# A decayed linear attention with two MLPs on one core: pair products by parity in row tiles of TensorE, and two operands turned by its transpose

## The chip, the core and the metric

The kernel runs on one core of one Trainium2 chip. The metric is the device time of one execution in microseconds (us); lower is better. Names used below: TensorE (PE in the profile; its weight loads are PEld), VectorE (DVE), ScalarE (ACT), GpSimd (POOL) and SyncE (SP), whose queue issues nearly all DMAs.

## What is computed

Attention first: for each of 4 x 8 heads a state of 40 x 40 goes through 768 tokens.

```python
for t in range(S):
    y[:, :, t] = np.einsum('bhd,bhde->bhe', rt, state)
    Sa = np.einsum('bhde,bhe->bhd', state, at)
    state_decay = state * wt[:, :, None, :] - np.einsum('bhd,bhe->bhde', Sa, bt)
    state = state_decay + np.einsum('bhd,bhe->bhde', vt, kt)
```

Then y, as 3072 rows of 320, goes through a first MLP, `((x @ w1) * (x @ w2)) @ w3 @ w_out` (width 1024), and a second, `h = x @ w_in; (h * cos(h)) @ w_out` (width 2048). All is float32.

## The kernel before

**Chunks.** The 768 tokens are cut into 24 chunks of C = 32. The 32 heads are kept as NP = 16 pairs: of each pair the even head lies on partitions 64 to 103 (the slice `EV`), the odd one on 0 to 39 (`OD`), D = 40 values of d each. "par" is 0 for even and 1 for odd. Four chunks make a group, whose small triangular systems are solved together.

**Preparation of a chunk** (`prep`, L313). On VectorE: a scan over the decays (L320), a product with k and b (L321, the tile KS, 104 partitions x 16 pairs x 64 columns: 32 of k and 32 of b), a reciprocal and a copy (L326, L327), a second scan (L329, Dp), and two products of a with it, one for each parity (L334), into the tile GA. GA holds, for each pair, 2 x 72 columns: for each parity 32 columns of the product and 40 of an identity, and zeros wherever the rows belong to the other parity. SyncE then issues the load of the next chunk's decays and a (`load_wa`, two DMAs, L282 and L283), and two DMAs that copy the products out of GA into the chunk's slot KA (L339).

**Pair products** (`gstage`, L342), in two halves of 8 pairs. L351: one matmul for each pair, stationary KS (104 rows, 64 columns), moving GA (104 rows, 144 columns). Because of GA's zeros each matmul gives both parities' 32 products, and, through the identity, k and b with tokens on rows. Results are in a PSUM tile PG, of two banks. ScalarE takes them out with 12 copies for each half (L361 into lam, the systems; L362 into KA; L363 into KB), and GpSimd masks KA (L369).

**v times r** (`mv`, L459): 16 matmuls for a chunk (L466), stationary v (104 rows, 32 columns), moving RD (104 rows, 2 x 32 columns, where the other parity's rows are zero). Copies to X (L472), masks (L475).

**The chain.** Chunk after chunk, in halves: `st_z` (L496), `st_q` (L513), `st_u` (L524), `st_y` (L542), `st_s` (L485), small float32 matmuls with copies and products between them on ScalarE, VectorE and GpSimd. It needs KA, KB and X of its chunk and the group's solved systems TT. Systems are solved by `tinv_start` (32 block transposes, L378) and `tinv` (L406, L408, L425, L428 on VectorE, with a share on GpSimd), and handed on by `tfin` (L457).

**The rest.** Between the pieces of the chain stand the first MLP's products (`ab`, L686), the folding of w3 and w_out (L586) and the conversion of weights from 64-bit words (L160 to L162). Phase 2 (`x2`, `hh`, `oo`, L736 to L798) follows.

**Order.** `attention` writes out the start by hand: chunks 0 to 3 are prepared and their systems solved, then chunks 4 and 5. From then on pieces are emitted by due times (`time`, constants START and PACE), which are their priorities too, and a list scheduler sets each engine's own order from that, with a model of its own for how long things take. Every engine then runs its list strictly in order, SyncE's queue too.

Of the kernel before, what the change touches and what calls it, by code (L numbers as in the profile page):

```python
# [9 lines left out]
F32 = mybir.dt.float32  # L10
# [42 lines left out]
def host_layout(inp):  # L53
# [20 lines left out]
    cst = np.zeros((128, 112 + NP * (C + 1)), np.float32)  # L74
    cst[OD, 0:D] = np.eye(D)
    cst[EV, 0:D] = np.eye(D)
    cst[:, 40:80] = 1.0
    cst[:, 80:112] = np.arange(128)[:, None] % 32 + np.arange(C)[None] >= C
    cst[:, 112::C + 1] = 1.0
# [15 lines left out]
class Room:  # L95
    """Buffers by tag, each in its turn, in places that something else has left."""
# [19 lines left out]
class Kernel:  # L116
# [25 lines left out]
    # ---------------------------------------------------------------- float64 words to float32  # L142
# [31 lines left out]
    # ---------------------------------------------------------------- attention  # L174
# [4 lines left out]
    def attn_open(self, ctx):  # L179
# [4 lines left out]
        self.ident_m = cp.tile([128, 112], F32, name="ident_m")  # L184
        self.ident = self.ident_m[:, 0:40]
        self.mask = self.ident_m[:, 80:112].unsqueeze(1)
        self.mask72 = self.ident_m[:, 40:112].unsqueeze(1)
# [10 lines left out]
        self.XX = t(104, [2, NP, 72], "Xe")  # L198
        self.X = [[self.XX[:, i] for i in range(2)], [t(128, [NP, 72], f"Xo{i}") for i in range(2)]]
# [11 lines left out]
    def prep_open(self):  # L211
# [21 lines left out]
        self.GA = [t(104, 2 * NP, 72).rearrange("p (x a) n -> p x a n", x=2), self.XX]  # L233

    def KS(self, c):
        """Of the first chunks in room that the weights will take, then in place."""
        if c >= PRE:
            return self.kb
        n = 2 * NP * C
        return self.ks[c // 2 % 2][0:104, n * (c % 2):n * (c % 2 + 1)].rearrange("p (a n) -> p a n", a=NP)  # L240

    def attn_init(self):
        nc = self.nc
        v, g, a = nc.vector, nc.gpsimd, nc.scalar
        nc.scalar.dma_start(out=self.d1r, in_=self.ap["cst"][0:104, 112:])
        nc.scalar.dma_start(out=self.ident_m, in_=self.ap["cst"][:, 0:112])
# [6 lines left out]
        idb = self.ident.unsqueeze(1)  # L253
        for t, e in zip(self.GA, (v, g)):
            e.memset(t, 0.0)
            a.copy(t[EV, 0, :, 32:72], idb[EV].to_broadcast([D, NP, D]))
            a.copy(t[OD, 1, :, 32:72], idb[OD].to_broadcast([D, NP, D]))
# [4 lines left out]
        for x in self.X[1]:  # L262
            g.memset(x, 0.0)
        for x in self.Dt:
            g.memset(x[32:64], 0.0)

    def attn_init2(self):
        nc = self.nc
        idb = self.ident.unsqueeze(1)
        for i in range(NB):  # L270
            nc.scalar.copy(self.KB[0][i][EV], idb[EV].to_broadcast([D, NP, D]))
            nc.scalar.copy(self.KB[1][i][OD], idb[OD].to_broadcast([D, NP, D]))
        nc.gpsimd.memset(self.XX, 0.0)
        nc.gpsimd.memset(self.RD, 0.0)
        nc.gpsimd.memset(self.vd[32:64], 0.0)
# [38 lines left out]
    def prep(self, c, alt=0):  # L314
# [3 lines left out]
        Dt, KS, GA = self.Dp, self.KS(c), self.GA[alt]  # L318
# [14 lines left out]
        for par, R in ((0, EV), (1, OD)):  # L333
            v.tensor_tensor(out=GA[R, par, :, 0:C], in0=self.a[R], in1=Dt[R], op=ALU.mult)  # L334
# [3 lines left out]
        for par, R in ((0, EV), (1, OD)):  # L338
            nc.sync.dma_start(out=self.KA[par][s][R], in_=GA[R, par, :, 0:C])  # L339
        yield  # L340

    def gstage(self, c, hf, alt=0, P=None):  # L342
# [3 lines left out]
        GA, KS = self.GA[alt], self.KS(c)  # L346
        for q in range(2):
            for e in range(2):
                for ct in range(2):
                    p = 8 * hf + 4 * q + 2 * ct + e  # L350
                    nc.tensor.matmul(P[64 * ct:64 * ct + 64, q, 144 * e:144 * e + 144], lhsT=KS[:, p, :], rhs=GA[:, :, p, :], start=True, stop=True)  # L351
        s, ci = c % NB, (c + OFF) % GC
        lam = self.lam.rearrange("p t (c f q e) -> p f q e t c", c=GC, f=2, q=2)
        pairs = lambda t: t[:, 8 * hf:8 * hf + 8].rearrange("p (q c e) n -> p c q e n", q=2, c=2)
        for ct in range(2):
            o = 64 * ct
            Pv = P[o:o + 64, :, 0:288].rearrange("p q (e x n) -> p x q e n", e=2, x=2)
            for par in range(2):
# [12 lines left out]
    def tinv_start(self):  # L371
        """Systems by partition: transpose blocks of lambda, and minus the identity."""
# [10 lines left out]
    def quads(t, row, col, *dims):  # L383
        """Both diagonal blocks of a matrix in halves, from a row and a column of the block on."""
        return bass.AP(tensor=t.tensor, offset=t.offset + 32 * row + 16 + col, ap=[t.ap[0], [496, 2], *dims])

    def tinv(self):
        """Minus the inverses, by halves of the tokens: both diagonal blocks by forward substitution, then the block
        between them as the product of the three; the first QD columns of a half on one engine, the others on another.
        Products before their sums lie in blocks of the systems that are done with."""  # L390
# [20 lines left out]
        def product(e, q0, q1, out, a, b):  # L411
            """out(q)[q, i], the sum over k of a[i, k] b(q)[q, k]."""
# [46 lines left out]
    def mv(self, c):  # L459
# [3 lines left out]
        for i in range(4):  # L463
            for ct in range(4):
                o = 288 + 64 * (i % 2)
                nc.tensor.matmul(P[32 * ct:32 * ct + 32, i // 2, o:o + 64], lhsT=self.vd[:, 4 * i + ct, :], rhs=RD[:, :, 4 * i + ct, :], start=True, stop=True)  # L466
        for ct in range(4):
            Pv = P[32 * ct:32 * ct + 32, :, 288:416].rearrange("p b (i x n) -> p x b i n", i=2, x=2)
            for par in range(2):
                o = 64 * par  # L470
                X = self.X[par][c % 2][o:o + 32, :, D:72].rearrange("p (b i c) n -> p c b i n", b=2, c=4)
                nc.scalar.copy(X[:, ct], Pv[:, par])  # L472
# [4 lines left out]
    def st_s(self, c, hf):  # L477
        """State rows by d for the next chunk's first stage, columns still to be scaled."""
# [128 lines left out]
    def w12(self, c):  # L607
        """256 columns of w1 and w2: both parts of two tiles of rows, and those of the 64 rows left over as one tile."""
# [40 lines left out]
    # ---------------------------------------------------------------- MLP  # L649
# [22 lines left out]
    def ab(self, s, x, f):  # L672
        """p for one tile of 128 hidden columns."""
# [33 lines left out]
    def load_p(self, s):  # L707
        """The parts of p, high and low."""
# [11 lines left out]
    def x2(self, s):  # L720
        """x2 by whole tiles of columns, then the rest with its two parts of weights as one tile."""
# [135 lines left out]
    def weights_b(self):  # L857
        """Weights of what follows, in the room of the attention's preparation."""
# [21 lines left out]
    def weights_c(self):  # L880
        """Weights of the last part, in the room of the last chunks as each ends."""
# [41 lines left out]
    def attention(self):  # L923
# [6 lines left out]
        for c in range(GC - OFF):  # L930
            for _ in self.prep(c, c % 2):
                pass
            for hf in range(2):
                self.gstage(c, hf, c % 2, halves[hf])
# [14 lines left out]
        for c in range(GC - OFF, PRE):  # L949
            for _ in self.prep(c):  # L950
                pass
            for hf in range(2):
                self.gstage(c, hf, 0, halves[hf])
# [52 lines left out]
    def back(self):  # L1006
        """The chunks' preparation, as far ahead as there is room, and each group's systems."""
# [89 lines left out]
```

## Time and profile before

| what | us |
|---|---|
| three runs | 1217.88, 1225.14, 1231.16 |
| median of the runs | 1225.14 |
| span of the profiled execution | 1225.8 |
| TensorE busy, of the span | 1054.0 |
| VectorE busy | 822.7 |
| ScalarE busy | 666.5 |
| GpSimd busy | 590.3 |
| mean granted TensorE clock | 0.919 of full speed |

The profiled execution thus stands 0.7 us above the median. A row of a group reads: line, engine, operation, tile written <- tiles read, shapes, count | busy us, mean ns of one | idle time before them and what ended it. A float32 matmul of the program stands in the trace as two matmuls and two weight loads; an fp32r matmul (the MLPs and the fold) as one. Ends of matmuls are modelled, with a latency of some 0.2 us in each, so starts are what paces are read from.

### The profile page before, as it was taken

The page shows a single profiled execution, that of the slowest core. Times are in us where ns is not written, and L with a number is a line of the kernel's source. Part 1 is how long each engine was busy: PE and PEld are TensorE (multiplying, and loading weights), DVE is VectorE, ACT ScalarE, POOL GpSimd, SP SyncE. Part 2 cuts the span into 40 slices and gives each one's busy share as a digit, 9 for nine tenths or more (in the row PEclk, how much of TensorE's full clock was granted, in tenths as well). Part 3 has the DMA queues.
Part 4 walks back from the last instruction along what each step waited for, and adds up shares of the span by engine and source line. Part 5 has one row for each costly group of instructions (what it writes and reads, how often), then busy time and mean ns, then how long its engine had stood idle before and what let it go on. Part 6 is the DMA issues. An engine that isn't in the chain of part 4 may idle for free. (4 is left out here: it accounts for less than half of the span.)

```text
span 1225.8 us, 34181 instructions
## 1 busy us (share of the span) xinstructions
PE 1054.0 (86%) x13536; PEld 954.3 (78%) x13536; DVE 822.7 (67%) x1774; ACT 666.5 (54%) x1750; POOL 590.3 (48%) x734
## 2 busy tenths in 40 slices
PE   2332558889999899999989999999999999999997
PEld 2322457767777777778877777899999999999997
DVE  5677799789769878976966666555455555455554
ACT  7653546646773765658435543455545555545453
POOL 7227557337345643734546654554334444334333
PEclk9755669899989999989989798999999999999999
DMA  5532545454554465454465545311101111101000
GB/s 133 137 86 67 144 118 150 136 145 116 162 144 123 129 159 148 118 160 119 136 202 160 142 140 166 119 35 46 46 21 37 46 36 47 45 20 38 12 4 20
DMA packets 137446, 122.96 MB, mean 100 GB/s; under 512 B 67293, under 2 KB 113885, under 8 KB 135749
## 3 DMA queue, kind: packets, MB, share of 16 engines
q1 hardware_dynamic: 137024, 120.49, 35.0%
q8 instruction: 106, 1.74, 0.6%
q14 instruction: 55, 0.45, 0.1%
q10 hardware_dynamic: 261, 0.28, 0.1%
HBM read 87.17 MB, written 29.62 MB: 95 GB/s over the span
## 5 line engine op out<-in xcount | busy, mean ns | idle before, releaser
L782 POOL TENSOR_TENSOR w<-w,w 128x512 fp32r<-128x512 f32 x96 | 126.1, 1321 | 224.8 <-ACT w L781 224.8
L686 PE MATMUL ab<-xh,w 128*128 128x256 f32 x960 | 177.7, 316 | 9.1 <-DVE p L691 8.5
L686 PEld LDWEIGHTS ab<-xh,w 128*128 128x128 f32 x960 | 135.7, 201 | 32.9 <-DVE p L691 10.1
L774 DVE SCALAR_TENSOR_TENSOR w<-w,h 128x512 f32<-128x512 int32 x96 | 65.7, 685 | 134.7 <-ACT w L772 120.0
L770 PE MATMUL h<-x2h,r 128*128 128x256 f32 x720 | 139.9, 280 | 1.3 <-ACT x2h L746 1.2
L776 ACT ACTIVATE w<-w,hpi 128x512 f32<-128x512 f32 x96 | 69.5, 724 | 93.1 <-DVE w L775 92.9
L770 PEld LDWEIGHTS h<-x2h,r 128*128 128x128 f32 x720 | 115.7, 188 | 1.8 <-ACT x2h L746 1.7
L778 DVE TENSOR_TENSOR w<-h,w 128x512 f32<-128x512 f32 x96 | 66.2, 689 | 65.5 <-ACT w L776 65.5
L361 ACT COPY sh<-PG 32x128 f32<-32x128 f32 x168 | 63.3, 377 | 50.9 <-PE PG L351 49.1
L690 ACT COPY p<-ab 128x256 f32<-128x256 f32 x96 | 35.8, 373 | 100.5 <-PE ab L686 85.5
L772 ACT ACTIVATE w<-h 128x512 int32<-128x512 f32 x96 | 57.1, 596 | 58.4 <-PE h L770 58.3
L775 DVE SCALAR_TENSOR_TENSOR w<-w 128x512 f32<-128x512 int32 x96 | 83.7, 871 | 3.3
L542 PE MATMUL PY<-Xe,r 104*40 104x72 f32 x768 | 69.3, 247 | 18.1 <-DVE Dt L554 9.6
L369 POOL TENSOR_SCALAR_AFFINE_SELECT r<-r 32x512 f32<-32x512 f32 x48 | 45.7, 952 | 79.7 <-ACT r L362 77.8
L686 PE MATMUL ab<-xl,w 128*128 128x256 f32 x384 | 82.2, 297 | 0.0
L770 PE MATMUL h<-x2l,r 128*128 128x256 f32 x288 | 79.8, 279 | 0.0
L781 ACT CAST w<-w 128x512 fp32r<-128x512 f32 x96 | 59.4, 619 | 34.6 <-DVE w L778 34.6
L542 PEld LDWEIGHTS PY<-Xe,r 104*40 104x40 f32 x768 | 58.1, 130 | 22.1 <-POOL Xe L533 6.1
L686 PE MATMUL ab<-xr,w 64*128 64x256 f32 x192 | 75.2, 395 | 0.0
L351 PE MATMUL PG<-sh 104*64 104x144 f32 x576 | 52.0, 322 | 22.2 <-issue 6.9
L542 PE MATMUL PY<-Xo,r 128*40 128x72 f32 x768 | 65.2, 246 | 1.3 <-POOL Xo L533 0.7
L686 PEld LDWEIGHTS ab<-xl,w 128*128 128x128 f32 x384 | 63.6, 203 | 1.0 <-issue 0.4
(218 smaller groups left out, 3428.3 us busy)
## 6 DMA issues: line engine op xcount, KB each, us to landing
pd<-p SPq DMA_DIRECT2D x96, 128.0 KB
sh<-wa SPq DMA_DIRECT2D x48, 242.5 KB
f<-w3t SPq DMA_DIRECT2D x32, 256.0 KB
sh<-kb SPq DMA_DIRECT2D x48, 160.0 KB
pl<-pd SPq DMA_DIRECT2D x6, 1024.0 KB
w<-pd SPq DMA_DIRECT2D x6, 1024.0 KB
w34d<-f SPq DMA_DIRECT2D x32, 160.0 KB
r<-wo SPq DMA_DIRECT2D x16, 320.0 KB
```

What stands on the lines that cost most here:

```text
L351: nc.tensor.matmul(P[64 * ct:64 * ct + 64, q, 144 * e:144 * e + 144], lhsT=KS[:, p, :], rhs=GA[:, :, p, :], start=True, stop=True)
L361: nc.scalar.copy(lam[32 * j:32 * j + 32, hf, :, :, :, ci], Pv[32:64, par, :, :, 0:C])
L542: nc.tensor.matmul(P[o:o + D, i // 4, 72 * (i % 4):72 * (i % 4) + 72], lhsT=self.KB[par][s][0:K, p, :], rhs=self.X[par][c % 2][0:K, p, :], ...
L686: nc.tensor.matmul(P[:, w], lhsT=l_, rhs=r_, start=(n == 0), stop=(n == len(ops) - 1))
L770: nc.tensor.matmul(P[:, q], lhsT=l_, rhs=r_, start=(n == 0), stop=(n == len(ops) - 1))
L772: a.activation(out=k, in_=P, func=ACTF.Copy, scale=1.0 / (2 * math.pi), bias=0.25)
L774: v.scalar_tensor_tensor(out=r, in0=k, scalar=-C1, in1=P, op0=ALU.mult, op1=ALU.add)
L775: v.scalar_tensor_tensor(out=r, in0=k, scalar=-C2, in1=r, op0=ALU.mult, op1=ALU.add)
L776: a.activation(out=r, in_=r, func=ACTF.Sin, bias=self.hpi)
L778: v.tensor_tensor(out=gt, in0=P, in1=r, op=ALU.mult)
L781: a.copy(gh, gt)
L782: g.tensor_tensor(out=gl, in0=gt, in1=gh.bitcast(F32), op=ALU.subtract)
```

## The change

`prep` writes a times Dp straight into the slot KA (contiguous rows of 40 x 512); GA, its zeros, its identities and the two copying DMAs (L339) go. `gstage` has two matmuls for a pair in place of one: the rows of one parity only (40 rows, 64 columns of KS, 32 columns moving), with the parities in different row tiles of TensorE and in different banks of PG. The identity part is replaced by four transposes in a half, each of two pairs of KS at once (104 rows x 128 columns in, 128 x 104 out, one 104 x 104 identity). `mv` likewise has 32 matmuls of 40 rows and 32 moving columns in place of 16 of 104 rows and 64. ScalarE's copies keep their number and sizes; they read other columns. At the start, GA's memsets and four identity copies go, X's zeros are set once.

```diff
@@ prep
-        for par, R in ((0, EV), (1, OD)):
-            v.tensor_tensor(out=GA[R, par, :, 0:C], in0=self.a[R], in1=Dt[R], op=ALU.mult)
+        for par, R in ((0, EV), (1, OD)):
+            v.tensor_tensor(out=self.KA[par][s][R], in0=self.a[R], in1=Dt[R], op=ALU.mult)
             if par == 0:
                 yield
         self.load_wa(c + 1)
-        for par, R in ((0, EV), (1, OD)):
-            nc.sync.dma_start(out=self.KA[par][s][R], in_=GA[R, par, :, 0:C])
@@ gstage
         for q in range(2):
             for e in range(2):
+                i = 2 * q + e
                 for ct in range(2):
                     p = 8 * hf + 4 * q + 2 * ct + e
-                    nc.tensor.matmul(P[64 * ct:64 * ct + 64, q, 144 * e:144 * e + 144], lhsT=KS[:, p, :], rhs=GA[:, :, p, :], start=True, stop=True)
+                    for par, R in ((0, EV), (1, OD)):
+                        nc.tensor.matmul(P[64 * ct:64 * ct + 64, par, C * i:C * i + C], lhsT=KS[R, p, :],
+                                         rhs=self.KA[par][s][R, p, :], start=True, stop=True)
+        for q in range(2):
+            for ct in range(2):
+                p = 8 * hf + 4 * q + 2 * ct
+                o = 128 + 104 * ct
+                nc.tensor.transpose(P[:, q, o:o + 104], KS[:, p:p + 2, :].rearrange("p a n -> p (a n)"), self.ident)
...
-                nc.scalar.copy(lam[32 * j:32 * j + 32, hf, :, :, :, ci], Pv[32:64, par, :, :, 0:C])
-                nc.scalar.copy(pairs(self.KA[par][s][r:r + 32])[:, ct], Pv[0:32, par, :, :, 0:C])
-                nc.scalar.copy(pairs(self.KB[par][s][r:r + 64])[:, ct], Pv[:, par, :, :, C:72])
+                nc.scalar.copy(lam[32 * j:32 * j + 32, hf, :, :, :, ci], Pv[32:64, par])
+                nc.scalar.copy(pairs(self.KA[par][s][r:r + 32])[:, ct], Pv[0:32, par])
+                nc.scalar.copy(odd(self.KB[par][s][r:r + 64])[:, ct], Pt[:, :, :, R])
@@ mv
         for i in range(4):
+            o = 336 + C * i
             for ct in range(4):
-                o = 288 + 64 * (i % 2)
-                nc.tensor.matmul(P[32 * ct:32 * ct + 32, i // 2, o:o + 64], lhsT=self.vd[:, 4 * i + ct, :], rhs=RD[:, :, 4 * i + ct, :], start=True, stop=True)
+                for par, R in ((0, EV), (1, OD)):
+                    nc.tensor.matmul(P[32 * ct:32 * ct + 32, par, o:o + C], lhsT=self.vd[R, 4 * i + ct, :], rhs=RD[R, par, 4 * i + ct, :], start=True, stop=True)
```

The list scheduler makes a new order of all this. Two engines and three places matter below.

SyncE, at the load of chunk 5's decays (`wa`, a DMA for each parity; `dtd` is Dp going out, r the slot that holds KA), before:

```order
L331 DMA dtd_99<-Dp 40x512 x2
L282 DMA sh_170<-wa 40x1552
L282 DMA vd<-vd 40x512
L309 DMA Xe<-vt 32x16x40 x2
L283 DMA vd<-vd 40x512
L304 DMA rd<-rd 40x512 x2
L283 DMA sh_170<-wa 40x1552
L339 DMA r<-sh_170 40x16x32 x2
```

and with the change:

```order
L315 DMA dtd_99<-Dp 40x512 x2
L266 DMA sh_171<-wa 40x1552
L267 DMA sh_171<-wa 40x1552
L266 DMA vd<-vd 40x512
L267 DMA vd<-vd 40x512
L288 DMA rd<-rd 40x512 x2
```

The second half of the load stood behind six other DMAs and now follows the first at once; the copies into the slot are gone.

VectorE, at the same time, from the block transposes of the first group's systems (x32) on, before:

```order
L378 STREAM_TRANSPOSE sh_171<-sh_170 128x32 x32
L406 TENSOR_TENSOR sh_171<-sh_171,sh_170 128x2x15
L408 TENSOR_TENSOR sh_170<-sh_170,sh_171 128x2x15
L406 TENSOR_TENSOR sh_171<-sh_171,sh_170 128x4x14
L408 TENSOR_TENSOR sh_170<-sh_170,sh_171 128x2x2x14
L406 TENSOR_TENSOR sh_171<-sh_171,sh_170 128x6x13
L408 TENSOR_TENSOR sh_170<-sh_170,sh_171 128x2x3x13
L320 SCALAR_TENSOR_TENSOR sh_170<-sh_170 104x528
```

and with the change:

```order
L371 STREAM_TRANSPOSE sh_172<-sh_171 128x32 x32
L304 SCALAR_TENSOR_TENSOR sh_171<-sh_171 104x528
L399 TENSOR_TENSOR sh_172<-sh_172,sh_171 128x2x15
L305 TENSOR_TENSOR w_176<-sh_171 104x2x16x32
L310 RECIPROCAL sh_172<-sh_171 104x16
L401 TENSOR_TENSOR sh_171<-sh_171,sh_172 128x2x15
```

The scan that waits for the load (L320, now L304) has moved ahead of six steps of the solution.

TensorE, at the 40th half of the pair products (the last but eight of all 48), before:

```order
L542 MATMUL PY<-Xe,r 40x72
L542 MATMUL PY<-Xo_147,r 40x72
L496 MATMUL PC_167<-rd,Ssb 40x64
L496 MATMUL PC_168<-rd,Ssb 40x64 x7
L351 MATMUL PG<-sh_170 64x144 x8
L496 MATMUL PC_168<-rd,Ssb 40x64
L586 MATMUL f<-f_751,f_753 128x320 x2
```

and with the change (L506 is `st_q`):

```order
L506 MATMUL PC_168<-Xe_147,r 32x72
L506 MATMUL PC_168<-Xo_149,r 32x72
L336 MATMUL PG<-r,sh_171 64x32 x16
L342 MATMUL PG<-ident,sh_171 128x104 x4
L506 MATMUL PC_169<-Xe_147,r 32x72
L506 MATMUL PC_169<-Xo_149,r 32x72
```

Eight matmuls of one shape have become sixteen and four, in two tilings of the array. Before, the neighbours L496 used the same tiling (all rows, 64 columns); now the tiling changes on entering, in the middle and on leaving.

More of the change, by code (lines that the diff above doesn't have):

```diff
@@ L73, in host_layout @@
     wf[..., 1:] = dmaj(w)[..., :-1]
[L74 to L79, printed above, removed]
+    cst = np.zeros((104, 104 + NP * (C + 1)), np.float32)
+    cst[:, 0:104] = np.eye(104)
+    cst[:, 104::C + 1] = 1.0
     return {
@@ L183, in attn_open @@
         self.ap_ = cp
[L184 to L187, printed above, removed]
+        self.ident = cp.tile([104, 104], F32, name="ident")
         t = lambda p, f, nm: cp.tile([p] + f, F32, name=nm)
@@ L197, in attn_open @@
         self.Dt = [t(104, [NP, C], f"Dt{i}") for i in range(ND)]
-        self.XX = t(104, [2, NP, 72], "Xe")
-        self.X = [[self.XX[:, i] for i in range(2)], [t(128, [NP, 72], f"Xo{i}") for i in range(2)]]
+        self.X = [[t(104, [NP, 72], f"Xe{i}") for i in range(2)], [t(128, [NP, 72], f"Xo{i}") for i in range(2)]]
         self.WC = [t(104, [NP], f"WC{i}") for i in range(NB + 1)]
@@ L244, in attn_init @@
         v, g, a = nc.vector, nc.gpsimd, nc.scalar
-        nc.scalar.dma_start(out=self.d1r, in_=self.ap["cst"][0:104, 112:])
-        nc.scalar.dma_start(out=self.ident_m, in_=self.ap["cst"][:, 0:112])
+        nc.scalar.dma_start(out=self.d1r, in_=self.ap["cst"][:, 104:])
+        nc.scalar.dma_start(out=self.ident, in_=self.ap["cst"][:, 0:104])
         v.memset(self.wa[32:64], 0.5)
@@ L252, in attn_init @@
         g.memset(self.lam, 0.0)
[L253 to L257, printed above, removed]
         for i in range(NB):
@@ L261, in attn_init @@
             g.memset(self.KB[1][i][0:64], 0.0)
-        for x in self.X[1]:
+        for x in self.X[0] + self.X[1]:
             g.memset(x, 0.0)
@@ L268, in attn_init2 @@
         nc = self.nc
[L269 removed]
         for i in range(NB):
[L271 to L273 removed]
+            for par, R in ((0, EV), (1, OD)):
+                nc.scalar.copy(self.KB[par][i][R], self.ident[R, R].unsqueeze(1).to_broadcast([D, NP, D]))
         nc.gpsimd.memset(self.RD, 0.0)
[L275 removed]
         for t in self.PC:
@@ L312, in load_vt, with prep @@
                 )
-    def prep(self, c, alt=0):
+    def prep(self, c):
         nc = self.nc
@@ L317, in prep @@
         s = c % NB
-        Dt, KS, GA = self.Dp, self.KS(c), self.GA[alt]
+        Dt, KS = self.Dp, self.KS(c)
         fl = lambda x: x.rearrange("p a t -> p (a t)")
@@ L337, in prep, with gstage @@
         self.load_wa(c + 1)
-        for par, R in ((0, EV), (1, OD)):
-            nc.sync.dma_start(out=self.KA[par][s][R], in_=GA[R, par, :, 0:C])
         yield
-    def gstage(self, c, hf, alt=0, P=None):
+    def gstage(self, c, hf, P=None):
         nc = self.nc
         P = P or self.PG
-        GA, KS = self.GA[alt], self.KS(c)
+        KS, s = self.KS(c), c % NB
         for q in range(2):
             for e in range(2):
+                i = 2 * q + e
                 for ct in range(2):
@@ L355, in gstage @@
         for ct in range(2):
             o = 64 * ct
-            Pv = P[o:o + 64, :, 0:288].rearrange("p q (e x n) -> p x q e n", e=2, x=2)
-            for par in range(2):
+            Pv = P[o:o + 64, :, 0:128].rearrange("p x (q e n) -> p x q e n", q=2, e=2)
+            Pt = P[o:o + 64, :, 128:336].rearrange("p q (c n) -> p q c n", c=2)
+            for par, R in ((0, EV), (1, OD)):
                 r = 64 * par
                 j = 2 * par + ct
-                nc.scalar.copy(lam[32 * j:32 * j + 32, hf, :, :, :, ci], Pv[32:64, par, :, :, 0:C])
-                nc.scalar.copy(pairs(self.KA[par][s][r:r + 32])[:, ct], Pv[0:32, par, :, :, 0:C])
-                nc.scalar.copy(pairs(self.KB[par][s][r:r + 64])[:, ct], Pv[:, par, :, :, C:72])
+                nc.scalar.copy(lam[32 * j:32 * j + 32, hf, :, :, :, ci], Pv[32:64, par])
+                nc.scalar.copy(pairs(self.KA[par][s][r:r + 32])[:, ct], Pv[0:32, par])
+                nc.scalar.copy(odd(self.KB[par][s][r:r + 64])[:, ct], Pt[:, :, :, R])
@@ L463, in mv @@
         for i in range(4):
+            o = 336 + C * i
             for ct in range(4):
-                o = 288 + 64 * (i % 2)
-                nc.tensor.matmul(P[32 * ct:32 * ct + 32, i // 2, o:o + 64], lhsT=self.vd[:, 4 * i + ct, :], rhs=RD[:, :, 4 * i + ct, :], start=True, stop=True)
+                for par, R in ((0, EV), (1, OD)):
+                    nc.tensor.matmul(P[32 * ct:32 * ct + 32, par, o:o + C], lhsT=self.vd[R, 4 * i + ct, :], rhs=RD[R, par, 4 * i + ct, :], start=True, stop=True)
         for ct in range(4):
-            Pv = P[32 * ct:32 * ct + 32, :, 288:416].rearrange("p b (i x n) -> p x b i n", i=2, x=2)
             for par in range(2):
                 o = 64 * par
-                X = self.X[par][c % 2][o:o + 32, :, D:72].rearrange("p (b i c) n -> p c b i n", b=2, c=4)
-                nc.scalar.copy(X[:, ct], Pv[:, par])
+                X = self.X[par][c % 2][o:o + 32, :, D:72].rearrange("p (i c) n -> p c i n", c=4)
+                nc.scalar.copy(X[:, ct], P[32 * ct:32 * ct + 32, par, 336:464].rearrange("p (i n) -> p i n", n=C))
         for par in range(2):
@@ L930, in attention @@
         for c in range(GC - OFF):
-            for _ in self.prep(c, c % 2):
+            for _ in self.prep(c):
                 pass
             for hf in range(2):
-                self.gstage(c, hf, c % 2, halves[hf])
+                self.gstage(c, hf, halves[hf])
         for _ in self.tinv_start():
@@ L952, in attention @@
             for hf in range(2):
-                self.gstage(c, hf, 0, halves[hf])
+                self.gstage(c, hf, halves[hf])
         self.ready |= {("tfin", 0), ("mv", 0)}
```

4 lines of the change are left out of this document (2 added, 2 removed).

## Prediction

> **What bounds the kernel now.** First the page's busy tenths in 40 slices of 30.6 us.
>
> ```profile
> PE   2332558889999899999989999999999999999997
> DVE  5677799789769878976966666555455555455554
> ACT  7653546646773765658435543455545555545453
> PEclk9755669899989999989989798999999999999999
> ```
>
> Three stretches show. In the first 120 us TensorE is a third busy at a low granted clock, and VectorE leads. From some 200 to 785 us TensorE is nearly full beside a busy VectorE. From 785 us on it is full, and the change touches nothing there. The stages in numbers (PE, PEld, DVE, ACT, POOL; clock; DMA):
>
> ```profile
> core 0: us, PE busy (x) PEld busy (x) DVE busy (x) ACT busy (x) POOL busy (x), PEclk, DMA share, GB/s
> 100.00:200.00 100.00, 52.95 (x1101) 46.33 (x1098) 84.34 (x224) 44.38 (x137) 61.68 (x92) 0.66 0.44 117
> 200.00:300.00 100.00, 87.61 (x1521) 73.30 (x1521) 85.68 (x221) 62.72 (x198) 52.00 (x77) 0.95 0.46 129
> 400.00:500.00 100.00, 90.04 (x1646) 75.23 (x1646) 82.72 (x216) 64.23 (x207) 48.08 (x69) 1.00 0.54 147
> 600.00:700.00 100.00, 91.54 (x1636) 76.84 (x1636) 67.17 (x148) 49.27 (x138) 62.80 (x91) 0.88 0.59 171
> 900.00:1000.00 100.00, 100.00 (x786) 99.96 (x785) 48.95 (x72) 52.12 (x93) 39.27 (x31) 1.00 0.14 43
> ```
>
> So in the middle TensorE's own time sets the end for nine tenths: a microsecond more or less on its list is worth about 0.9. At the start it is VectorE's list up to the first solved systems, for which the chain waits (total, times, longest, in us):
>
> ```profile
> PEld PC L524 <- DVE TT L457: 15.7, 1, 15.7
> ```
>
> **TensorE's paces.** Its list around 406 to 413 us (start, length, count), and the v-times-r products at 654 us:
>
> ```profile
> 406.04 1.20 PE L351 MATMUL PG<-sh 104*64 104x144 f32 x16
> 411.13 0.73 PE L524 MATMUL PC<-Q,TT 32*32 32x72 f32 x32 [1.54 <-ACT Q L515]
> 412.19 0.75 PE L686 MATMUL ab<-xh,w 128*128 128x256 f32 x5
> 412.78 0.40 PE L686 MATMUL ab<-xl,w 128*128 128x256 f32 x2
> 413.11 0.38 PE L686 MATMUL ab<-xr,w 64*128 64x256 f32 x1
> 413.42 0.50 PE L686 MATMUL ab<-xh,w 128*128 128x256 f32 x2
> 654.69 0.65 PE L466 MATMUL PG<-rd,vd 104*32 104x64 f32 x32
> ```
>
> Durations, minimum/median/maximum in ns, and when the group ran:
>
> ```profile
> L351 PE MATMUL PG<-sh x576: 283/286/503, 83.5 to 571.3; 104*64 104x144 f32 x192
> L351 PEld LDWEIGHTS PG<-sh x576: 132/137/231, 83.4 to 571.2; 104*64 104x64 f32 x192
> L513 PEld LDWEIGHTS PC<-Xe,r x768: 106/110/178, 62.0 to 717.2; 104*32 104x32 f32 x192
> L524 PE MATMUL PC<-Q,TT x1536: 221/221/329, 115.5 to 723.7; 32*32 32x72 f32 x192
> L686 PEld LDWEIGHTS ab<-xh,w x960: 186/188/338, 185.1 to 776.6; 128*128 128x128 f32 x192
> L466 PE MATMUL PG<-rd,vd x768: 216/219/317, 53.2 to 695.8; 104*32 104x64 f32 x192
> ```
>
> Taking the last one's latency off a run and dividing by the steps: L351 (1.20 - 0.29) / 15 = 61 ns a record, L524 (0.73 - 0.22) / 31 = 16 ns, L466 (0.65 - 0.22) / 31 = 14 ns. L351 uses two tiles of 64 columns in turn, the others four tiles. If tiles run beside each other, one record takes 121 ns for 144 moving columns, 66 for 72, 56 for 64: always 0.84 to 0.91 ns a column. 32 columns should take 28 ns. A weight load grows from 110 ns at 32 columns to 188 at 128, 0.81 ns a column: 52 ns for 64 columns, 104 for 128, if the rest is latency. In the full array an fp32r record goes at (412.78 - 412.19) / 5 = 0.118 us for 256 columns. From the first xl to the 64-row xr it is 0.33 us, so the second xl took 0.21: a **change of tiling** costs 0.09 us.
>
> **The change on TensorE, half by half.** Removed: 16 records at 61 ns, 0.97 us.
>
> Added, products: 32 records in four tiles (two row tiles, two column tiles), eight rounds. A round takes 28 ns if the streams decide (0.22 us in all), 52 if the 64-column loads do (0.42), and 16 rounds of 52 if two row tiles over the same columns don't run together (0.83). L524's four tiles lie on a diagonal, so no row shows row tiles sharing columns. I take 0.42: loads must go on, and L351's gaps have never tested one that is longer than its stream.
>
> Added, transposes: four with 128-column loads. The trace has none. From below, 104 columns at the full array's pace, 48 ns each (0.19 us); from above, two records each like other float32 work here, both load-bound (8 x 104 = 0.83). I take one record, load-bound, 0.42, as L686's 32-bit words go in one record. The Trainium skill ("TensorE: Matmul & The Clock Gate", Terms) has a transpose mode four times as fast for float32; by it the 0.42 would stand, and no run so far shows one.
>
> So a half takes 0.84 (0.41 to 1.66) for 0.97. From 83 to 571 us there are 576 / 16 = 36 halves: -4.7 us (-20 to +25).
>
> **v times r.** Now 32 records x 14 ns = 0.45 us a chunk. Then 64 records of 28 ns: 0.45 if four run at once, as now, 0.22 if all eight tiles do, 64 x 14 = 0.90 if the 14 ns are a price of each record. I take 0.45: nothing (for some 20 chunks in the middle, -5 to +9 us).
>
> **Tilings.** The transposes stand in the full array between products in 64 x 64 tiles, and `st_s`, `st_y`, `st_z` no longer share a tiling with them. Counted over TensorE's order from the first `st_q` to the last `st_y`, the tiling changes 590 times before and 696 times after. 106 x 0.09 = +9.5 us.
>
> Together +4.8 us on TensorE (-25 + 9.5 = -15 at best, +25 + 9 + 9.5 = +43 at worst). At 0.9 of it: **+4.3 us** (-14 to +39).
>
> **The change at the start.** VectorE's list around the first systems (brackets: idle before, and what ended it):
>
> ```profile
> 57.86 3.07 DVE L378 STREAM_TRANSPOSE sh<-sh 128x32 f32<-128x32 f32 x32
> 65.65 1.26 DVE L320 TENSOR_TENSOR_SCAN sh<-sh 104x528 f32<-104x528 f32 x1 [3.04 <-DMA sh<-wa]
> 76.77 1.26 DVE L320 TENSOR_TENSOR_SCAN sh<-sh 104x528 f32<-104x528 f32 x1 [2.12 <-DMA sh<-wa]
> 88.36 1.26 DVE L320 TENSOR_TENSOR_SCAN sh<-sh 104x528 f32<-104x528 f32 x1 [2.94 <-DMA sh<-wa]
> 101.49 1.26 DVE L320 TENSOR_TENSOR_SCAN sh<-sh 104x528 f32<-104x528 f32 x1 [2.56 <-DMA sh<-wa]
> 113.57 1.90 DVE L457 STREAM_TRANSPOSE TT<-sh 128x1024 f32<-128x1024 f32 x1
> ```
>
> And SyncE's queue, start and length of each issue, at the load that the first of these scans waits for:
>
> ```profile
> 56.86 0.30 SPq L282 DMA_DIRECT2D sh<-wa  x1
> 57.26 0.79 SPq L282 DMA_DIRECT2D vd<-vd  x1
> 60.91 0.28 SPq L283 DMA_DIRECT2D sh<-wa  x1
> 61.24 1.73 SPq L339 DMA_DIRECT2D r<-sh  x2
> ```
>
> The scans wait 10.7 us there. The first is late because the load's second half is issued at 60.91, behind vd, vt and rd; scan and issue lie 4.7 us apart. With the halves side by side it starts near 57.3 + 4.7 = 62.0, one microsecond after the transposes end (60.9) and not three to five. The fourth scan now has the rest of the first solution step and five products of the next ahead of it, which cover its load. The two between keep their waits. That leaves 1 + 2.1 + 2.9 + 0 = 6 of 10.7 us, so TT is ready **5 us** earlier (0 to 7: GpSimd's share of the solution might be what is late next), and VectorE, 84% busy until 200 us, hands it on.
>
> **Costed at nothing.** The copies L339 took 1.73 us of SyncE's queue for a chunk; no compute instruction in the middle waited for them, and they were not on the way to the end. VectorE's product keeps its size. GA's memsets and identities lie under the first load of decays. ScalarE's copies read as many columns. If SyncE's relief does help, it is a microsecond or two.
>
> Sum: 1225.8 + 4.3 - 5 = **1225 us**, within 0.1 us of the runs' median of 1225.1. The likeliest case's own range is 1214 to 1237; a measurement of this kernel tells about 1% (12 us) from no change.
>
> **Rivals.**
>
> *Row tiles overlap and little else costs (chance 0.25).* Streams decide, not loads, transposes go at the full array's pace, eight tiles run at once: -14 us on TensorE's list as above, -5 at the start, so 1207. For it: the paces fit streams everywhere. Against: the tiling changes are certain.
>
> *TensorE pays by the record (0.20): slower.* The place is the stream of short records in `gstage` and `mv`: 32 and 64 records where 16 and 32 stood. If products go two at a time behind 64-column loads (0.83) and `mv` keeps 14 ns a record (0.90), then (0.83 + 0.42 - 0.97) x 36 = +10, +9 and +9.5: 28.5 x 0.9 - 5 = +21, so 1246. It decides from some 20 ns a product record on. For it: no record here goes below 14 ns on average. Against: 14 and 16 ns fit streams of 56 and 66 ns in four tiles.
>
> The Trainium skill ("TensorE: Matmul & The Clock Gate", the section "Wait — 56ns, not 53.3ns?") states that starts never follow closer than about 25 ns. As a rule for all tiles together (0.03) it would make 32 x 25 = 0.80 and 64 x 25 = 1.6 us: +9, +23 and +9.5, times 0.9, less 5: 1258. L524's 16 ns and L466's 14 ns speak against it.
>
> *It does not reach the end (0.10).* TensorE's list isn't what binds where the halves stand, since VectorE is 80% busy beside it; only the start counts: 1221, still no change.
>
> **How the numbers follow.** Forecast 0.42 at 1225, hidden 0.10 at 1221: no change beyond 1% (1213 to 1237) has 0.52. Faster has 0.25, slower 0.20 + 0.03 = 0.23. The range takes in the first two rivals, 1206 to 1248.
>
> **What would show it.** Right: a half's products near 0.4 us plus latency and four transposes near 0.4; `mv` still near 0.65 us; 100 more changes of tiling; the transposition into TT (L457 before) near 108 us; phase 2 as long as before. Wrong: products at 1 us a half, eight transpose records a half, `mv` above 1 us, or TT when it was. A span that moves with none of these would mean that the new order, and not these costs, decides.

## The result, and the profile after

The changed kernel takes 1288.1 us in the median of four runs (1275.4 to 1293.4), the kernel before 1228.2 us beside it (1217.9 to 1237.2). The ratio is 1.047, with a 95% interval of 1.041 to 1.054: slower by 60 us, where 1225 us was forecast and 1248 was the end of the range. Here and below medians are over all runs of a kernel and ratios over its fast runs alone, so the two can differ by some tenths of a per cent.

Where the time lies is seen in the busy tenths of the changed kernel's page, now slices of 32.3 us.

```profile
PE   2433468988987998989998989999999999999997
DVE  4677797589668676875766557535555445555554
PEclk9999557799986998987969889799999999999999
```

The attention's last `st_y` ends at 801 us, 734 before, and what follows takes 491 us, 492 before, in the two profiled executions of 1291 and 1226 us: all of the loss is ahead of phase 2. From the 7th slice to the 26th the granted clock has a digit under 9 in 11 slices, down to 6; before it had one in 6, down to 7. Stage by stage (columns as before: PE, PEld, DVE, ACT, POOL; clock; DMA):

```profile
100.00:200.00 100.00, 51.88 (x1091) 44.51 (x1091) 85.07 (x222) 41.35 (x125) 59.06 (x90) 0.67 0.39 108
200.00:300.00 100.00, 89.57 (x1703) 75.02 (x1704) 73.06 (x193) 53.03 (x171) 34.15 (x53) 0.85 0.41 122
400.00:500.00 100.00, 91.59 (x1636) 76.33 (x1633) 70.00 (x151) 55.30 (x175) 38.04 (x64) 0.89 0.42 119
600.00:700.00 100.00, 95.40 (x1748) 80.57 (x1747) 65.89 (x189) 51.63 (x152) 40.75 (x74) 0.84 0.39 115
900.00:1000.00 100.00, 100.00 (x786) 99.95 (x785) 52.16 (x76) 53.44 (x95) 43.85 (x34) 1.00 0.12 39
```

The clock fell from 0.95, 1.00 and 0.88 to 0.85, 0.89 and 0.84 in the three middle stages. TensorE is as busy as before, or busier, but slower. The attention, from the first `tfin` (113 us before, 112 after) to the last `st_y` (734 and 801), first before, then after:

```profile
113.00:734.00 621.00, 540.23 (x9518) 453.96 (x9519) 489.80 (x1249) 359.54 (x1105) 329.11 (x488) 0.90 0.51 141
```

```profile
112.00:801.00 689.00, 586.38 (x10900) 490.44 (x10900) 495.46 (x1258) 361.67 (x1110) 316.45 (x489) 0.83 0.43 125
```

So TensorE idles 102.6 us instead of 80.8, and at a clock of 0.83 instead of 0.90 the rest takes longer too. What TensorE waited for in these stretches (total, times, longest in us), before and then after:

```profile
PE PC L513 <- DVE Xo L502: 19.6, 13, 7.0
PE PY L542 <- DVE Dt L554: 9.6, 5, 5.9
```

```profile
PE PC L506 <- DVE Xo L495: 25.5, 11, 7.5
PE PY L535 <- DVE Dt L547: 23.9, 10, 6.9
```

Both are the chain's hand-overs from VectorE: `st_q` waits for what `st_z` left, `st_y` for room in PY. They cost 20 us more. The pieces of the change themselves are nearly as small as forecast. The first two rows below are a half's products and its transposes, the third is v times r, all at full clock (start, length, count):

```profile
305.60 0.67 PE L336 MATMUL PG<-r,sh 40*64 40x32 f32 x32
306.20 0.58 PE L342 MATMUL PG<-ident,sh 104*128 104x104 f32 x4
247.20 0.76 PE L460 MATMUL PG<-rd,vd 40*32 40x32 f32 x64
```

### The profile page after: what moved, and what is told of

Its sections match the earlier page's. It is cut to its first block, busy times and chain, and to the rows that moved or that the text cites. A ratio compares the mean times of both kernels' runs of the same rounds, so it can differ in the third digit from the quotient of the medians.

```text
span 1291.3 us, 37565 instructions
## 1 busy us (share of the span) xinstructions
PE 1102.8 (85%) x15264; PEld 990.6 (77%) x15264; DVE 821.4 (64%) x1773; ACT 664.5 (51%) x1746; POOL 572.3 (44%) x733
## 4 chain that ended last, share of the span: by engine, by line
PE 46%; DVE 20%; DMA 13%; issue 10%; POOL 5%; ACT 4%; SPq 1%; POOLq 0%; DVEq 0%; ACTq 0%
PE ab L679 11%; PE h L763 10%; DMA sh<-wa 4%; PE o L791 3%; PE o L790 3%; PE o L789 3%; POOL w L775 3%; PE PC L506 2%; DVE r L318 2%; PE PY L535 2%; PE x L731 1%; PE x L729 1%; DMA f<-w 1%; PE x L730 1%; DVE sh L418 1%
## 5 line engine op out<-in xcount | busy, mean ns | idle before, releaser
L679 PE MATMUL ab<-xh,w 128*128 128x256 f32 x960 | 190.4, 333 | 8.4 <-DVE p L684 6.2
L679 PEld LDWEIGHTS ab<-xh,w 128*128 128x128 f32 x960 | 146.9, 217 | 36.0 <-DVE p L684 7.9
L679 PE MATMUL ab<-xl,w 128*128 128x256 f32 x384 | 87.5, 313 | 0.0
L362 POOL TENSOR_SCALAR_AFFINE_SELECT r<-r 32x512 f32<-32x512 f32 x48 | 41.4, 862 | 101.3 <-ACT r L355 99.6
L679 PE MATMUL ab<-xr,w 64*128 64x256 f32 x192 | 79.8, 417 | 0.0
L169 POOL TENSOR_TENSOR f<-f,f 128x256 fp32r<-128x256 f32 (+1 forms) x48 | 37.7, 788 | 91.6 <-ACT f L168 81.6
L684 DVE TENSOR_TENSOR p<-ab,p 128x256 f32<-128x256 f32 x96 | 40.1, 419 | 60.0 <-ACT p L683 55.0
L506 PE MATMUL PC<-Xe,r 104*32 104x72 f32 x768 | 49.0, 265 | 25.6 <-DVE Xo L495 25.5
```

What stands on the lines that cost most here:

```text
L506: nc.tensor.matmul(P[32 * j:32 * j + 32, 72 * k:72 * k + 72], lhsT=self.KA[par][s][0:K, p, :], rhs=self.X[par][c % 2][0:K, p, :], start=Tr ...
L679: nc.tensor.matmul(P[:, w], lhsT=l_, rhs=r_, start=(n == 0), stop=(n == len(ops) - 1))
```

## The experiments

The trace offers two causes: the new instructions (more of them, in more tilings, and perhaps so little work for the array that the clock falls), or the new order that the list scheduler made of the whole program, since the due times and the scheduler's rules were left as they were. The first shall be called the instruction theory, the second the order theory.

To tell them apart, an order must be put on other instructions. The instructions were matched one by one: the k-th of a function on an engine in one kernel is the k-th in the other; a product of the old form stands for two records of the new, and the four transposes follow the last product of their half. A table then chains what each engine issues, with edges that order it and wait for nothing:

```diff
         Kernel(tc, ap, out).run()
+        hold(tc, nc, ORDER)
...
+def hold(tc, nc, order):
...
+        for x, y in zip(ranks, ranks[1:]):
+            tc.add_manual_dep(by[e][y], by[e][x].name, info, reason="order")
```

Where a dependency of the instructions forbids a place, the row moves back to the first place that is allowed.

### Orders and instructions exchanged

**e1, the changed kernel's instructions in the order of the kernel before.**

> The changed kernel's instructions, each engine held to the order that the kernel before has (16 row-tile products where 8 products stood, the four transposes behind them, 32 records for 16 in v times r). The order theory (the new order makes the stalls and these the half clock) expects the kernel before plus some 5 to 15 us: ratio 1.00 to 1.015, half-clock time near that of before (110 to 140 us between 130 us and the end of the attention). The instruction theory (the row tiles, the transposes and the changes of tiling themselves, or the clock that so little work of the array is granted) expects the time of the changed kernel: ratio 1.035 to 1.055, half-clock time 200 us and more.

Measured: 1266.0 us, ratio 1.033 (1.029 to 1.038). Between the two theories; but the first systems were transposed at 136 us instead of 112, because the order at the start did not suit the new start. From there the attention took 634 us, against 620 before and 688 with the change.

**e2, the instructions of the kernel before in the changed kernel's order.**

> The other corner: the instructions of the kernel before, each engine held to the changed kernel's order. The order theory expects most of the loss without any of the new instructions: ratio 1.03 to 1.055. The instruction theory expects no change: ratio 0.995 to 1.01. If both corners are slow by 3% or more, neither is right alone: an order fits the durations it was made for.

Measured: 1345.4 us, 1.098 (1.090 to 1.106). Old instructions in the new order are far slower, and not a new record is there. It isn't a clean corner: the start is late by the same 23 us, and the 48 copies L339 have no place in the new order and stand right behind the outgoing Dp. The late start explains 23 of the 119 us; from there the attention took 713 us. By the letter both corners are slow by over 3%, the third reading of the expectation: an order fits the instructions it was made for. Without the late starts e1 comes near the order theory, with 14 us, and e2 loses more than that theory expected, with 93.

**e3, v times r alone in row tiles, and e4, the pair products and transposes alone,** each with an order of the scheduler's own.

```diff
 # e3, in the kernel before
...
-                nc.tensor.matmul(P[32 * ct:32 * ct + 32, i // 2, o:o + 64], lhsT=self.vd[:, 4 * i + ct, :], rhs=RD[:, :, 4 * i + ct, :], start=True, stop=True)
+                for par, R in ((0, EV), (1, OD)):
+                    nc.tensor.matmul(P[32 * ct:32 * ct + 32, par, o:o + C], lhsT=self.vd[R, 4 * i + ct, :], rhs=RD[R, par, 4 * i + ct, :], start=True, stop=True)
...
```

```diff
 # e4, in the changed kernel (mv as before, its results at 336 and not at 288)
-            o = 336 + C * i
             for ct in range(4):
-                for par, R in ((0, EV), (1, OD)):
-                    nc.tensor.matmul(P[32 * ct:32 * ct + 32, par, o:o + C], lhsT=self.vd[R, 4 * i + ct, :], rhs=RD[R, par, 4 * i + ct, :], start=True, stop=True)
+                o = 336 + 64 * (i % 2)
+                nc.tensor.matmul(P[32 * ct:32 * ct + 32, i // 2, o:o + 64], lhsT=self.vd[:, 4 * i + ct, :], rhs=RD[:, :, 4 * i + ct, :], start=True, stop=True)
...
```

> The kernel before with v times r alone in row tiles (32 records of 32 columns for 16 of 64), the order left to the scheduler. The instruction theory expects +2 to +6 us from the records (ratio 1.00 to 1.005). The order theory gives no sign: any ratio from 0.99 to 1.05, and a departure of over 10 us either way would be more than the instructions can cost.

> The changed kernel with v times r as before (its results moved right by 48 columns, clear of the transposes), the order left to the scheduler. The instruction theory expects nearly the whole loss here: ratio 1.035 to 1.05. The order theory gives no sign: any ratio from 0.99 to 1.05; one below 1.015 would say that the products and transposes cost little by themselves.

Measured: e3 1257.3 us, 1.026 (1.022 to 1.031); e4 1269.4 us, 1.041 (1.032 to 1.050). Each half of the change loses on its own; together they lose less than the sum. The 31 us of e3 are far more than its records can cost, so this smallest edit was taken apart next.

### The same two by two, cleanly

Between the kernel before and e3 every instruction has its counterpart, and no row had to move back.

**e6, v times r in row tiles, in the order of before, and e7, the kernel before in the order of e3.**

> v times r alone in row tiles, every engine held to the order of the kernel before (each of the 16 records becomes two, one behind the other; nothing else is moved). The order theory expects +0 to +8 us (ratio 1.00 to 1.007), where the same instructions in the scheduler's new order took 1.026. The instruction theory expects 1.02 to 1.03 again.

> The kernel before, not one instruction changed, in the order that the scheduler made when v times r alone was in row tiles. The order theory expects that run's loss: ratio 1.015 to 1.03. The instruction theory expects 0.995 to 1.005.

Measured: e6 1225.8 us, 1.001 (0.997 to 1.005); e7 1251.4 us, 1.020 (1.016 to 1.024). The new records cost nothing in the old order; the old records lose 2.0 of the 2.6% in the new one. For this part the order theory holds. e7's row for the attention shows the same picture as the change, with instructions that are the old ones to the last, and below it stands what TensorE waits for:

```profile
114.00:762.00 648.00, 546.71 (x9535) 458.72 (x9535) 490.54 (x1259) 361.42 (x1110) 327.73 (x490) 0.89 0.49 137
```

```profile
PE PC L513 <- DVE Xo L502: 22.4, 15, 6.5
PE PY L542 <- DVE Dt L554: 20.3, 11, 6.9
```

Idle TensorE went from 80.8 to 101.3 us, and 13.5 of these 20.5 us are in the same two waits.

**e5 and e9, e1 with a start that suits it.** e5 is held to the old order only from the first `tfin` on. e9 keeps the changed kernel's own order up to the end of chunk 0 and has the old one from there.

> The first run again, but held to the old order only from the first group's transposed systems on: holding it from the start had put these at 136 us instead of 112. The order theory expects them at 112 us again and the rest as in that run: ratio 1.005 to 1.02 (1233 to 1250 us). The instruction theory expects the changed kernel's time: 1.035 to 1.055.

> The changed kernel's instructions in their own order up to the end of chunk 0, and from there in the order of the kernel before; so the start should lie where the changed kernel has it (first transposed systems at 112 us, 122 in the run held from there on). The order theory expects the whole loss to be gone: ratio 0.998 to 1.008 (1225 to 1238 us), the attention about 5 us longer than before. If what the held run of 1.017 lost was not its late start but the instructions: 1.012 to 1.02. The instruction theory in its first form: 1.035 or more.

Measured: e5 1247.6 us, 1.017 (1.010 to 1.025), its first systems still late, at 122 us. e9 1231.8 us beside 1232.0 for before: 0.999 (0.994 to 1.003). With the start at 110 us and the old order behind it, all of the changed kernel's instructions take the time of the kernel before. Its row, and the two waits:

```profile
110.00:731.00 621.00, 548.50 (x10879) 460.02 (x10880) 489.51 (x1249) 359.95 (x1105) 323.81 (x487) 0.89 0.48 137
```

```profile
PE PY L535 <- DVE Dt L547: 16.4, 6, 6.6
PE PC L506 <- DVE Xo L495: 11.8, 8, 5.8
```

TensorE is busy 8 us more than before, and idles 8 us less (72.5 for 80.8); the two waits make 28 us, 29 before and 49 with the change. Half of the 8 us is the one wait for the first systems, first before, then in e9:

```profile
PE PC L524 <- DVE TT L457: 15.2, 1, 15.2
```

```profile
PE PC L517 <- DVE TT L450: 11.0, 1, 11.0
```

**The whole loss of 4.7% is the order's:** the same instructions take 1.047 in one order and 0.999 in the other. Every held run orders all engines at once; which engine's order does the harm was not taken apart.

### Is TensorE's time worth anything here?

**e12, e9 with each transpose issued twice.**

```diff
-        for q in range(2):
+        for q in (0, 1, 0, 1):
             for ct in range(2):
...
                 nc.tensor.transpose(
```

> As the ninth run, with each of the four transposes of a half issued twice to the same place (the same values): some 4 x 0.12 us in each of 38 halves of chunks, 15 to 18 us of TensorE's time in the attention. If TensorE's own time sets the end for nine tenths, as the prediction had it: the ninth run plus 13 to 17 us. If it falls into idle time of TensorE: the ninth run plus 0 to 5 us.

Measured: 1228.3 us, 0.9995 (0.996 to 1.003), which is e9's time (0.999) within the noise of some 0.6%. The added transposes do stand on TensorE's list. Groups of e9 and then e12, duration ns minimum/median/maximum, first and last start:

```profile
L342 PE MATMUL PG<-ident,sh x144: 252/253/433, 80.2 to 572.0; 104*128 104x104 f32 x144
```

```profile
L342 PE MATMUL PG<-ident,sh x288: 252/253/433, 80.4 to 579.1; 104*128 104x104 f32 x144
```

From 110 us on the time from a transpose's start to the next start on TensorE, without the few behind which it stood idle, sums to 16.6 us in e9 and 30.4 in e12: some 14 us of added work. At 0.9 that would be 12.5 us, or 1.0%, at the end; the end moved by 0.1%. But the added work did not fall into idle time, as the expectation had it. e12's row for the attention:

```profile
110.00:737.00 627.00, 555.31 (x11013) 466.99 (x11014) 487.90 (x1249) 360.03 (x1105) 328.85 (x487) 0.91 0.47 136
```

TensorE idles 71.7 us, 72.5 in e9, and the attention is 6 us longer. What paid for most of the work is the granted clock, 0.91 for 0.89: 112.6 us at half clock instead of 133.1, worth 10 us. Over the runs the clock's median is 0.951 in e12 and 0.938 in e9. So more work on the list left the end where it was, within the noise, but these traces do not show it as fill of gaps.

### Is the order of before special, and where does a bad one lose?

**e8, e13, e14: the kernel before with another `PACE`** (18650, 18100 and 19100 ns a chunk for 18598), **and e15, e16: the changed kernel with 18100 and 19100.** No instruction changes.

```diff
-START, PACE = 69126, 18598
+START, PACE = 69126, 18100
```

> The kernel before with one constant of its due times 0.3% larger (18650 ns a chunk for 18598), which moves 1493 of TensorE's rows by a few places and changes no instruction. If the order of before is a picked one among many worse (the order theory in its wide form): ratio 1.01 to 1.04. If only some orders are bad and the change hit one by chance: within 1%.

> The kernel before with due times 2.7% closer (18100 ns a chunk), which moves 3954 of TensorE's rows by 7.9 places in the mean, as far as the change moved them (7.5). If the constants were picked for the kernel before and any order that far from it is worse: ratio 1.01 to 1.04. If moving rows that far is harmless in itself: 0.995 to 1.01.

> The same the other way (19100 ns a chunk; 3770 rows by 10.6 places in the mean). Picked constants: 1.01 to 1.04. Harmless: 0.995 to 1.01.

> The changed kernel with 18100 ns a chunk. If its 1.047 is one draw among the orders that the scheduler makes, and others are better: a ratio that differs from 1.047 by 0.015 or more to either side, more likely below. If every order that the scheduler makes for the new instructions is as bad: 1.04 to 1.055.

> The changed kernel with 19100 ns a chunk. One draw among orders: differs from 1.047 by 0.015 or more. All as bad: 1.04 to 1.055.

| kernel | order | ratio (95%) |
|---|---|---|
| before | PACE 18650 | 1.002 (0.998 to 1.006) |
| before | PACE 18100 | 1.016 (1.011 to 1.022) |
| before | PACE 19100 | 1.029 (1.017 to 1.041) |
| changed | as given, 18598 | 1.047 (1.041 to 1.054) |
| changed | PACE 18100 | 1.054 (1.046 to 1.063) |
| changed | PACE 19100 | 1.057 (1.047 to 1.067) |

Both readings hold in part. A small step in the constant is harmless, so the order theory in its widest form (any other order loses) falls. Orders as far from the old one as the change's are 1.6 and 2.9% slower with the old instructions: of the four orders that this scheduler made for them, the order of before and its near neighbour are the good ones. But three orders for the new instructions all lose 5%, and e15 and e16 differ from 1.047 by 0.007 and 0.010, not by the 0.015 expected of a mere draw (1.057 lies just above the range expected where all are as bad). Why the scheduler orders the new instructions worse than it does the old ones is not settled; that it prices the short records too dear is a guess that no run tried.

**e10 and e11, the kernel before in the order of e3 only up to the end of chunk 3, or only from there on.**

> The kernel before, instructions unchanged, in the order of the third run up to the end of chunk 3 and in its own from there on. In the third order chunk 3 ended 17 us later than before, and the whole kernel 28 us. If time lost by the chain of chunks at one place is not made up later: ratio 1.010 to 1.016. If later slack takes it back: below 1.005.

> The complement: the kernel before in its own order up to the end of chunk 3 and in the order of the third run from there on. If losses at separate places add: ratio 1.004 to 1.010. If the loss is in that order wherever it is used: 1.015 to 1.022.

Measured: e10 1245.9 us, 1.016 (1.010 to 1.023); e11 1261.6 us, 1.026 (1.021 to 1.031). The end of each chunk's last `st_y` on VectorE in us, and how much later it came in the others:

| chunk | before | change | e7 | e10 | e11 | e9 |
|---|---|---|---|---|---|---|
| 0 | 135.8 | -1.4 | -0.1 | +0.7 | -0.6 | -3.1 |
| 3 | 215.0 | +17.7 | +17.0 | +19.6 | +0.6 | -1.4 |
| 7 | 324.0 | +13.6 | +14.2 | +19.1 | +17.7 | +1.8 |
| 11 | 436.2 | +28.5 | +14.5 | +19.9 | +22.9 | +2.8 |
| 15 | 537.0 | +40.7 | +26.0 | +18.9 | +28.8 | +0.1 |
| 19 | 646.9 | +53.0 | +14.2 | +21.5 | +17.3 | -2.9 |
| 23 | 733.8 | +66.7 | +28.1 | +17.4 | +31.8 | -2.7 |

e10 loses 20 us in its first four chunks and has not got them back after twenty chunks of the old order. Time can be won back in another order, though: e7 and e11 stand 26.0 and 28.8 us behind at chunk 15 and 14.2 and 17.3 at chunk 19. e11 fell out with both readings of its expectation: freed of those 17 us, it loses as much between chunks 3 and 7. Losses don't add by places, and a single bad spot isn't the cause.

What such a place looks like, in chunk 2 on TensorE; before, then the change, from `st_q` (L513, L506) to `st_u` of the first half (L524, L517), at half clock in both:

```profile
161.53 0.33 PE L513 MATMUL PC<-Xe,r 104*32 104x72 f32 x1
...
163.34 1.19 PE L524 MATMUL PC<-Q,TT 32*32 32x72 f32 x32 [0.61 <-ACT Q L515]
```

```profile
164.82 0.33 PE L506 MATMUL PC<-Xe,r 104*32 104x72 f32 x1 [3.00 <-DVE Xo L495]
...
166.42 0.28 PE L460 MATMUL PG<-rd,vd 40*32 40x32 f32 x2 [0.39 <-DMA rd<-rd]
...
167.99 0.95 PE L460 MATMUL PG<-rd,vd 40*32 40x32 f32 x62
...
169.48 1.32 PE L517 MATMUL PC<-Q,TT 32*32 32x72 f32 x32
```

Before, `st_u` starts 1.8 us behind `st_q`. Now v times r of the next chunk and the second half's `st_q` stand ahead of it, the former waits 0.39 us for its load, and `st_u` starts 4.7 us behind.

### Where the lost time goes

From the records of each trace, one execution of each kernel: the attention's length, TensorE's idle time in it, the time at half of the full clock, and what is left when the idle time and half of the half-clock time are taken off (us).

| kernel | attention | idle | at half clock | left |
|---|---|---|---|---|
| before | 620.2 | 80.2 | 122.1 | 479.0 |
| e9 | 620.9 | 72.2 | 133.1 | 482.2 |
| e12 | 627.3 | 72.1 | 112.6 | 498.9 |
| e7 | 648.2 | 101.6 | 146.8 | 473.2 |
| e14 | 659.0 | 86.1 | 197.0 | 474.4 |
| change | 688.5 | 102.6 | 228.7 | 471.6 |

TensorE's work at full clock is much the same in all but e12, where its transposes were doubled. What differs is idle time and clock: for the change 22 us of idle time and 107 / 2 = 53 us by the clock, of the 68 us that the attention got longer (some of the idle time is counted twice). The table splits the time; no run held the clock and changed the order alone, so how far the one brought on the other is an argument (the last section has the windows for it). But the clock does not follow from the new instructions: e9 has them all and 11 us more at half clock than before, the change 107.

## Why the prediction was wrong, point by point

**The step that failed** is a term that the sum put at nothing: it held the order as it was. The prediction worked with the new order at the start and with its changes of tiling, and took the rest to be as good as the old; its last sentence named the other possibility ("would mean that the new order, and not these costs, decides") and gave it no chance and no price. The same instructions take 0.999 of the time before in the old order (e9) and 1.047 in the new one: the term is worth +60 us. With it went the clock: the prediction's rows show it at 0.95, 1.00 and 0.88 in the middle, no term let it fall, and 53 of the attention's 68 us go with time at half clock.

**A second step failed with it:** "in the middle TensorE's own time sets the end for nine tenths: a microsecond more or less on its list is worth about 0.9". A row of 0.91 busy was read as a bound at a fixed clock. e12 put 14 us on that list and the end moved by 0.1%, not 1.0, and in its trace the clock rose. Alone this step would have cost little: the sum had only 4.8 us to multiply. What sets the end instead is not shown in full. The waits that grow with a bad order are the chain's hand-overs from VectorE, with the first MLP's products laid between its pieces, but in e12 the idle time stayed as it was.

**The terms of the sum** were right in mechanism and nearly in size. Products: (0.67 - 0.22) / 31 = 14.5 ns a record, 0.46 us a half for the 0.42 taken. Transposes: one record each, as taken, (0.58 - 0.25) / 3 = 109 ns apart for 104. v times r: (0.76 - 0.20) / 63 = 8.9 ns a record, 0.57 us for the 0.45 taken, so the eight tiles run neither at the half nor at the full price. Tilings: 696 changes, as counted. In the old order all of it together is worth nothing that the runs can tell: what TensorE's work takes at full clock grew by 3 us from before to e9 (482.2 for 479.0), where the sum had 4.8, and e9's ratio of 0.994 to 1.003 has room for the forecast's 1225 us as well as for the 1221 of the rival "it does not reach the end".

**The start** gained 1.5 us, not 5. VectorE's list around the first systems, now:

```profile
58.15 3.07 DVE L371 STREAM_TRANSPOSE sh<-sh 128x32 f32<-128x32 f32 x32
62.95 1.26 DVE L304 TENSOR_TENSOR_SCAN sh<-sh 104x528 f32<-104x528 f32 x1 [1.74 <-DMA sh<-wa]
73.83 1.26 DVE L304 TENSOR_TENSOR_SCAN sh<-sh 104x528 f32<-104x528 f32 x1 [2.35 <-DMA sh<-wa]
85.74 1.26 DVE L304 TENSOR_TENSOR_SCAN sh<-sh 104x528 f32<-104x528 f32 x1 [2.96 <-DMA sh<-wa]
101.09 1.24 DVE L304 TENSOR_TENSOR_SCAN sh<-sh 104x528 f32<-104x528 f32 x1
112.03 1.90 DVE L450 STREAM_TRANSPOSE TT<-sh 128x1024 f32<-128x1024 f32 x1
```

The waits behaved as forecast: 7.0 us for the 6 forecast, from 10.7, with the last one gone. But between the two transpositions VectorE was busy 45.1 us instead of 43.3, with the same 112 instructions. Shown are the two stretches, before first:

```profile
57.86:113.57 55.71, 16.97 (x208) 14.54 (x208) 43.27 (x112) 23.64 (x88) 26.39 (x40) 0.53 0.35 85
```

```profile
58.15:112.03 53.88, 18.19 (x378) 14.73 (x378) 45.09 (x112) 23.43 (x86) 23.13 (x40) 1.00 0.23 72
```

The step took VectorE's instructions to keep their lengths, and in the new order they are longer; why, no run here shows. What the start is worth at the end the runs can't tell for so few microseconds: e9, with its first systems 3.3 us earlier than before, ends within an interval of 5 us to either side. A start 23 us late did reach the end, in e1 (39 us longer in all, 14 of them in the attention).

**The other rivals.** "TensorE pays by the record" came nearest by its sign and wasn't the cause: it decides from 20 ns a product record on, and 14.5 were measured. The same goes for the 25 ns from start to start of the Trainium skill ("TensorE: Matmul & The Clock Gate", the section "Wait — 56ns, not 53.3ns?"): across row and column tiles starts follow at 14.5 and 8.9 ns here.

## What to carry to other kernels

A TensorE that is 90% busy in a stage need not set the end there microsecond for microsecond; the test is to lay some work more on it, see whether the end moves, and look in the trace whether idle time or the clock paid for it. Where a list scheduler and tuned due times set the order, an edit's first effect can be the new order: put the old order on the new instructions before judging them by the time, and count a new order as a term of its own when forecasting an edit to a tuned kernel (here the scheduler's orders cost from nothing to 6%, and none gained). Idle time that an order costs can be followed by half clock, which here took more than the idle time itself (53 us beside 22).

## What the runs showed of the hardware

**The granted clock falls without a long pause.** The matmul records were counted in windows of 3.41 us, in step with the clock's changes, over the attention before and after. At full clock, 34 windows had TensorE busy under 60%, and 31 of them were followed by half clock; of 12 between 60 and 70% two were; 230 were 70% busy or more, and none was. From half clock, none of 30 windows under 80% was followed by full clock, and only 30 of 61 that were over 95% busy. A stretch of the changed kernel shows both (PE busy first, granted clock third from the right):

```profile
639.00:642.41 3.41, 1.36 (x37) 1.16 (x37) 3.14 (x11) 0.41 (x1) 0.00 (x0) 1.00 0.11 36
642.41:645.83 3.42, 3.42 (x42) 2.83 (x37) 3.13 (x10) 0.43 (x1) 1.72 (x4) 0.50 0.28 65
645.83:649.24 3.41, 3.41 (x14) 2.74 (x13) 3.22 (x11) 0.00 (x0) 2.83 (x9) 0.50 0.61 165
649.24:652.65 3.41, 3.41 (x12) 2.74 (x13) 2.22 (x6) 0.37 (x1) 2.99 (x5) 0.50 0.45 130
652.65:656.07 3.42, 3.42 (x51) 2.51 (x57) 1.30 (x4) 0.37 (x1) 1.29 (x3) 0.50 0.04 13
656.07:659.48 3.41, 3.41 (x76) 2.89 (x75) 1.88 (x4) 2.46 (x9) 0.65 (x1) 0.50 0.47 142
659.48:662.89 3.41, 3.41 (x41) 2.78 (x40) 0.41 (x2) 0.37 (x1) 1.55 (x4) 0.50 0.60 186
662.89:666.30 3.41, 3.41 (x44) 2.69 (x35) 2.62 (x10) 1.13 (x3) 0.92 (x2) 0.50 0.12 38
```

Two microseconds of idle time in one window were followed by seven windows at half clock, in all of which TensorE was fully busy: 24 us, in which 12 us of work at full clock were lost. The Trainium skill ("TensorE: Matmul & The Clock Gate", the section "What's actually happening") gives the window's length, 3.4 us, as seen here, and has one busy window lift the clock; here half of them did not. Its rule for kernels, no idle gap over some 3.4 us (the section "HAM oscillation — how this bites in real kernels"), is too mild for this chain, where 1.1 to 3.4 us of idle time within one window sufficed. What decides when a busy window lifts the clock, these traces do not show.
